# Running the first three weight blocks of an MLP over one half of the rows before the other half

## The chip, the cores and the metric

The kernel runs on one core of a Trainium2 chip. The metric is the device time of one execution in microseconds (us), as the median of several runs. The core has a matrix engine (TensorE, PE in the tables; its weight loads are listed apart as PEld), VectorE (DVE), ScalarE (ACT), GpSimd (POOL), and SyncE (SP), which issues the DMA transfers. Every engine works through its own queue in order.

## The reference

Four batches of 768 tokens with 384 features go through an attention-like recurrence, a real 2-D Fourier mix with layer norm, and two MLPs. Cut to what matters, for each batch:

```
y  = recurrence(q, k, v, a)                 # the scan and its attention form
u  = x + real(fft2(x))                      # x is y with its heads merged
un = layer_norm(u)
u  = u + relu(un @ w_ch1) @ w_ch2           # first MLP, 384 -> 1536 -> 384
u  = u + (relu(u.T @ w_tok1) @ w_tok2).T    # mix over the tokens
u  = u + relu(u @ w3) @ w4                  # second MLP, no layer norm
```

All is float32 at the interface. Each matrix is held as a high and a low part, and a product is three matmuls (high by high, low by high, high by low).

## The kernel before

Each batch is done by two strands of work. The **chain** is the scan (`scan`, mostly small VectorE steps and TensorE transposes at L642), the attention chunks (L753 to L810), and `stage2` (Fourier matmuls L1028 and L1039, the residual add L1091, layer norm L1098 to L1120). The **dense** strand is `mlp` (first MLP), `tok1` and `tok2` (the mix over tokens), `transposed`, and `mlp` again (second MLP). While the dense strand of batch b runs, the chain of batch b + 1 runs beside it. For batch 0 there is nothing to run beside the end of its chain. In the first dense pass the weights are also converted from the input form (`convert`, L185 to L207), which loads VectorE, GpSimd and ScalarE.

The program writes the strands one after the other with a priority on every instruction, and the scheduler that builds the program merges them into one fixed order for each engine, from these priorities and from what it takes to be ready. On TensorE the chain goes first and the dense work fills in; on VectorE, ScalarE and GpSimd the dense work goes first, conversions next, and the chain last. In each queue that order then holds, whatever the chip does.

A batch's 768 rows are six tiles of 128 rows. Layer norm finishes them in pairs: tiles 0 and 3, then 1 and 4, then 2 and 5 (L1118 on ScalarE, L1120 on VectorE). `transposed` takes them in the order 0, 3, 1, 4, 2, 5: three TensorE transposes for a tile (L906) into a PSUM bank of tag "s" (three banks), a ScalarE copy into the high part `th` (L909), and a VectorE subtraction for the low part `tl` (L910). `th` and `tl` have two halves of three tiles; before the change, half 0 holds tiles 0, 1, 2 and half 1 holds tiles 3, 4, 5.

`mlp` has four quarters. In a quarter, each of three weight blocks makes two groups of nine matmuls (L926), one for each half of the rows (384 columns); each group is evicted from a PSUM bank of tag "l" (three banks) by a ScalarE relu (L930) and a VectorE subtraction (L939), or for some by a second ScalarE relu and a GpSimd subtraction (L936, L937). Then six row tiles each take nine matmuls with the second weights (L948) and are added to `u` on VectorE (L951). Each weight tile is in one of four buffers for its tag ("w1" or "w2"), loaded at L283 in a fixed list. The hidden tiles `h` have three buffers.

The last batch is not run in that pattern: there the first MLP of batch 3 is interleaved with the token mix of batch 2 (`mixed`), and that stretch has no chain beside it any more.

Of the kernel before, what the change touches and what calls it, by code (L numbers as in the profile page):

```python
# [9 lines left out]
F32R = mybir.dt.float32r  # L10
I32 = mybir.dt.int32
U32 = mybir.dt.uint32
ACTF = mybir.ActivationFunctionType
# [40 lines left out]
def attn_fft_mixer_kernel(ctx: ExitStack, tc: tile.TileContext, aL, xL, vL, wL, qN, kN, vN, arN, aiN,  # L54
# [37 lines left out]
    def alloc(tag, shape, dt=F32, name=None):  # L92
        n = 1
        for x in shape[1:]:
            n *= x
        t = pool.tile([128, SIZE[tag]], dt, tag=tag, bufs=BUFS[tag], name=name or tag)
        return shaped(t[0:shape[0], 0:n], shape)
# [3 lines left out]
    def palloc(tag, shape):  # L101
        n = 1
        for s in shape[1:]:
            n *= s
        t = psum.tile([128, 512], F32, tag=tag, bufs=PSB[tag], name=tag)
        v = t[0:shape[0], 0:n]
        if len(shape) == 3:
            v = v.rearrange("p (a b) -> p a b", b=shape[2])
        return v

    def r32(ap):
        return ap.bitcast(F32)
# [786 lines left out]
    def transposed(u, un, pt):  # L899
        th = [alloc("T", [128, 3, 384], F32R, name="th") for _ in range(2)]  # L900
        tl = [alloc("T", [128, 3, 384], F32R, name="tl") for _ in range(2)]
        for i in range(6) if un is None else (0, 3, 1, 4, 2, 5):
            src = u[i] if un is None else un[:, i, :]
            px = palloc(pt, [128, 3, 128])
            for dt in range(3):
                te.transpose(px[:, dt, :], src[:, dt * 128:dt * 128 + 128], ident)  # L906
            o = (i % 3) * 128
            hi = th[i // 3][:, :, o:o + 128]
            se.copy(out=hi, in_=px)  # L909
            ve.tensor_tensor(out=tl[i // 3][:, :, o:o + 128], in0=px, in1=r32(hi), op=ALU.subtract)  # L910
        return th, tl

    def mlp(u, b, p0, th, tl, done):
        for qd in range(4):
            hs = []
            for m in range(3):
                p = p0 + 3 * qd + m
                w1 = ws.get(b, p, 0)
                h = alloc("h", [128, 2, 768], F32R, name="h")
                hs.append(h)  # L920
                for g in range(2):
                    ps = palloc("l", [128, 384])
                    n = 0
                    for kt in range(3):
                        for wi, x in ((0, th), (0, tl), (1, th)):
                            te.matmul(out=ps, lhsT=w1[:, wi, kt * 128:kt * 128 + 128],  # L926
                                      rhs=x[g][:, kt, :], start=(n == 0), stop=(n == 8))
                            n += 1
                    hi = h[:, 0, g * 384:g * 384 + 384]
                    x = se.activation(out=hi, in_=ps, func=ACTF.Relu)  # L930
                    marked(x)
                    lo = h[:, 1, g * 384:g * 384 + 384]
                    if done is None and 0 < b < B - 1 and m < 2:

                        full = alloc("f", [128, 384], name="full")
                        se.activation(out=full, in_=ps, func=ACTF.Relu)  # L936
                        ge.tensor_tensor(out=lo, in0=full, in1=r32(hi), op=ALU.subtract)  # L937
                    else:
                        ve.scalar_tensor_tensor(out=lo, in0=ps, scalar=0.0, in1=r32(hi), op0=ALU.max, op1=ALU.subtract)  # L939
                ws.ensure(b, p, 0, 2)  # L940
                yield True
            for tt in range(6):
                ps = palloc("l", [128, 384])
                n = 0
                for m in range(3):
                    w2 = ws.get(b, p0 + 3 * qd + m, 1)
                    for hi, wi in ((0, 0), (0, 1), (1, 0)):
                        te.matmul(out=ps, lhsT=hs[m][:, hi, tt * 128:tt * 128 + 128], rhs=w2[:, wi, :],  # L948
                                  start=(n == 0), stop=(n == 8))
                        n += 1  # L950
                ve.tensor_tensor(out=u[tt], in0=u[tt], in1=ps, op=ALU.add)  # L951
                if done is not None and qd == 3:
                    done(tt)
# [218 lines left out]
                    n += 1  # L1172
            ve.tensor_tensor(out=u[tt], in0=u[tt], in1=ps, op=ALU.add)

    def dense1(b, u, th, tl):
        go(mlp(u, b, 0, th, tl, None))
        R = tok1(b, u)
        tok2(b, u, *R)
        return transposed(u, None, "l")

    def mlp2(b, u, th, tl, row=None):
        def done(tt):
            sp.dma_start(out=out[b if row is None else bass.ds(row, 1), tt], in_=u[tt])
        return mlp(u, b, 16, th, tl, done)

    def dense2(b, u, th, tl, row=None):
        go(mlp2(b, u, th, tl, row))

    def mixed(g, b, u):

# [32 lines left out]
        u = u1  # L1223
    u1, norm = on(CHAIN, chain, B - 1)
    t3 = on(CHAIN, transposed, u1, norm, "s")
    on(DENSE, go, mlp(u, B - 2, 0, *t1, None))
    t2 = mixed(mlp(u1, B - 1, 0, *t3, None), B - 2, u)
    t3 = mixed(mlp2(B - 2, u, *t2), B - 1, u1)
    go(mlp2(B - 1, u1, *t3))

# [122 lines left out]
```

## Time and profile before

| what | value |
|---|---|
| median of 3 runs | 1102.06 us (1101.85 to 1102.67) |
| span of the profiled execution | 1097.6 us |
| time of the runs outside such a span (1102.06 - 1097.6) | 4.46 us |
| TensorE busy | 981.1 us, 89% |
| VectorE busy | 776.3 us, 71% |
| ScalarE busy | 511.7 us, 47% |
| GpSimd busy | 420.9 us, 38% |

The span runs from the first to the last instruction of one profiled execution. Busy shares are means over stages that have different limits, so they say only which engines are candidates. A matmul's end is modelled, so that its listed duration (some 0.33 us) is longer than the spacing of matmuls in a row.

### The profile page before, as it was taken

What the parts mean: (1) busy time and instruction counts of PE and PEld (TensorE: products, weight loads), DVE (VectorE), ACT (ScalarE), POOL (GpSimd) and SP (SyncE); (2) the same over time, 40 slices, a digit from 0 to 9 for tenths busy, and PEclk for the clock granted to TensorE, in tenths of its full rate; (3) what the DMA queues carried; (4) which work ended last, traced back from release to release, by engine and by line L of the source; (5) the groups of instructions that cost most, each with busy time, mean ns of one, the idle gap of its engine ahead of it and who ended that gap; (6) DMA issues with size and microseconds to landing.
All of it is one profiled execution on the core that took longest, in us unless ns stands there. A gap on an engine that the chain in (4) does not pass through costs nothing.

```text
span 1097.6 us, 21079 instructions
## 1 busy us (share of the span) xinstructions
PE 981.1 (89%) x7314; PEld 919.2 (84%) x7314; DVE 776.3 (71%) x2083; ACT 511.7 (47%) x1425; POOL 420.9 (38%) x552
## 2 busy tenths in 40 slices
PE   1358797999889989799998999999897999999997
PEld 0227675989889887799997899999786999999997
DVE  6986987999999668999758879984744433433332
ACT  6753355777877225968315556842234212121111
POOL 6643985573576454345336312424512002000000
PEclk9997797999999999799999999999998999999999
DMA  6136954686758663356664346664303433443432
GB/s 217 45 82 180 298 175 152 220 272 196 233 182 274 201 185 124 110 165 180 158 192 147 107 138 194 186 184 131 122 29 115 144 116 130 159 154 127 165 101 75
DMA packets 101537, 174.66 MB, mean 159 GB/s; under 512 B 11056, under 2 KB 61104, under 8 KB 100912
## 3 DMA queue, kind: packets, MB, share of 16 engines
q1 hardware_dynamic: 101424, 173.24, 51.1%
q8 instruction: 60, 0.98, 0.4%
q14 instruction: 53, 0.43, 0.1%
HBM read 133.88 MB, written 39.32 MB: 158 GB/s over the span
## 4 chain that ended last, share of the span: by engine, by line
PE 64%; DVE 10%; ACT 2%; DMA 2%; issue 1%; POOL 1%; SPq 0%; POOLq 0%; DVEq 0%; ACTq 0%
PE l L948 23%; PE l L926 21%; PE s L753 3%; PE s L642 2%; PE s L1039 2%; PE s L802 2%; DVE ws L994 2%; PE s L1028 1%; PE s L808 1%; PE s L1153 1%; PE s L768 1%; DVE ws L988 1%; PE s L1171 1%; DVE cvt L199 1%; PE s L906 1%
## 5 line engine op out<-in xcount | busy, mean ns | idle before, releaser
L948 PE MATMUL l<-w,h 128*128 128x384 f32 x1728 | 326.8, 340 | 5.7 <-DVE h L939 5.1
L926 PE MATMUL l<-th,w 128*128 128x384 f32 x1152 | 317.2, 344 | 8.8 <-DVE u L951 5.0
L948 PEld LDWEIGHTS l<-w,h 128*128 128x128 f32 x1728 | 298.4, 189 | 10.0 <-DVE h L939 7.2
L926 PEld LDWEIGHTS l<-th,w 128*128 128x128 f32 x1152 | 212.9, 191 | 13.3 <-DVE u L951 6.3
L926 PE MATMUL l<-tl,w 128*128 128x384 f32 x576 | 196.0, 340 | 3.6 <-DVE tl L910 3.6
L930 ACT ACTIVATE h<-l 128x384 fp32r<-128x384 f32 x192 | 94.0, 490 | 212.7 <-PE l L926 212.0
L951 DVE TENSOR_TENSOR u<-u,l 128x384 f32<-128x384 f32 x192 | 105.3, 549 | 81.9 <-PE l L948 80.9
L939 DVE SCALAR_TENSOR_TENSOR h<-l,h 128x384 fp32r<-128x384 f32 x160 | 88.4, 553 | 88.5 <-ACT h L930 88.3
L926 PEld LDWEIGHTS l<-tl,w 128*128 128x128 f32 x576 | 110.1, 191 | 4.1 <-DVE tl L910 4.1
L196 POOL TENSOR_TENSOR cvt<-cvt 128x384 int32<-128x384 int32 x56 | 64.7, 1160 | 36.7 <-DVE cvt L194 11.0
L466 PE MATMUL s<-misc,y 128*112 128x128 f32 x96 | 21.7, 369 | 53.1 <-DVE y L444 48.8
L466 PEld LDWEIGHTS s<-misc,y 128*112 128x112 f32 x96 | 14.0, 177 | 62.3 <-issue 26.8
L753 PE MATMUL s<-qkt 112*96 112x96 f32 x512 | 59.2, 266 | 6.7 <-DVE sc L760 6.7
L753 PEld LDWEIGHTS s<-qkt 112*96 112x96 f32 x512 | 53.2, 177 | 9.4 <-DVE sc L760 7.4
L1138 POOL TENSOR_TENSOR xl<-u,xh 128x384 fp32r<-128x384 f32 x18 | 17.9, 1006 | 105.6 <-ACT xh L1137 105.6
L206 POOL TENSOR_TENSOR w<-cvt,w 128x384 fp32r<-128x384 f32 x44 | 51.2, 1172 | 9.9 <-ACT w L205 6.1
L199 DVE SCALAR_TENSOR_TENSOR cvt<-cvt 128x384 int32<-128x384 int32 x56 | 48.1, 865 | 7.0 <-POOL cvt L196 6.8
L571 POOL TENSOR_TENSOR tm<-tm 128x144 f32<-128x144 f32 (+1 forms) x51 | 27.1, 531 | 59.0 <-ACT tm L570 58.7
L937 POOL TENSOR_TENSOR h<-full,h 128x384 fp32r<-128x384 f32 x32 | 33.6, 1049 | 35.5 <-ACT full L936 33.7
L642 PE MATMUL s<-misc,y 128*112 128x128 f32 x288 | 45.0, 276 | 1.4 <-DVE y L626 1.0
L615 DVE TENSOR_TENSOR p<-p,A 128x144 f32<-128x144 f32 x144 | 44.6, 310 | 2.2
L786 POOL TENSOR_TENSOR yc<-Aa,gm 48x384 f32<-48x384 f32 x18 | 21.0, 1164 | 63.3 <-DVE Aa L779 63.3
(234 smaller groups left out, 1950.8 us busy)
## 6 DMA issues: line engine op xcount, KB each, us to landing
w<-wscr SPq DMA_DIRECT2D x180, 384.0 KB, 3.5
cvt<-wL SPq DMA_DIRECT2D x56, 384.0 KB, 4.6
wscr<-w SPq DMA_DIRECT2D x44, 384.0 KB, 3.5
Kn<-kn SPq DMA_DIRECT2D x64, 192.0 KB, 3.7
kn<-y SPq DMA_DIRECT2D x96, 96.0 KB, 2.5
raw<-aL SPq DMA_DIRECT2D x48, 144.0 KB, 3.2
xx<-xL SPq DMA_DIRECT2D x48, 144.0 KB, 3.1
V<-vL SPq DMA_DIRECT2D x32, 144.0 KB, 3.1
```

What stands on the lines that cost most here:

```text
L196: x = ge.tensor_tensor(out=a, in0=a, in1=lo, op=ALU.add)
L199: rest(ve.scalar_tensor_tensor(out=a, in0=hi, scalar=-0x80000000, in1=a, op0=ALU.bitwise_and, op1=ALU.bitwise_or))
L206: ge.tensor_tensor(out=parts[:, 1, :], in0=a.bitcast(F32), in1=r32(parts[:, 0, :]), op=ALU.subtract)
L466: te.transpose(ps[:, j, :], y[:, j, 0:112], ident)
L615: ve.tensor_tensor(out=cur, in0=prev, in1=A[:, j, 0:3, :], op=ALU.mult)
L642: te.transpose(ps[:, j, :], y[:, j, 0:112], ident)
L753: te.matmul(out=ps[:, j, :], lhsT=K[:, hc, :], rhs=Q[:, hc, :])
L926: te.matmul(out=ps, lhsT=w1[:, wi, kt * 128:kt * 128 + 128], rhs=x[g][:, kt, :], start=(n == 0), stop=(n == 8))
L930: x = se.activation(out=hi, in_=ps, func=ACTF.Relu)
L939: ve.scalar_tensor_tensor(out=lo, in0=ps, scalar=0.0, in1=r32(hi), op0=ALU.max, op1=ALU.subtract)
L948: te.matmul(out=ps, lhsT=hs[m][:, hi, tt * 128:tt * 128 + 128], rhs=w2[:, wi, :], start=(n == 0), stop=(n == 8))
L951: ve.tensor_tensor(out=u[tt], in0=u[tt], in1=ps, op=ALU.add)
```

## The change

`transposed` fills the halves in the order in which layer norm delivers the tiles: where it follows layer norm, half 0 now holds tiles 0, 3, 1 and half 1 holds tiles 4, 2, 5. It also returns the `u` tiles in that order, and `mlp` adds its result to them in that order. With `halves=True` (the first MLP of batches 0, 1 and 2) the first quarter of `mlp` runs half 0 through its three weight blocks, and then half 1 through the same three blocks; the three hidden tiles are taken at its start. The first MLP of batch 3 keeps its order of blocks, with the new order of tiles. The numbers of matmuls, evictions, weight loads and stores stay as they are.

```diff
     def transposed(u, un, pt):
...
-        for i in range(6) if un is None else (0, 3, 1, 4, 2, 5):
+        order = range(6) if un is None else (0, 3, 1, 4, 2, 5)
+        for j, i in enumerate(order):
...
-            o = (i % 3) * 128
-            hi = th[i // 3][:, :, o:o + 128]
+            o = (j % 3) * 128
+            hi = th[j // 3][:, :, o:o + 128]
             se.copy(out=hi, in_=px)
-            ve.tensor_tensor(out=tl[i // 3][:, :, o:o + 128], in0=px, in1=r32(hi), op=ALU.subtract)
-        return th, tl
+            ve.tensor_tensor(out=tl[j // 3][:, :, o:o + 128], in0=px, in1=r32(hi), op=ALU.subtract)
+        return [u[i] for i in order], th, tl
 
-    def mlp(u, b, p0, th, tl, done):
+    def mlp(b, p0, u, th, tl, done, halves=False):
+        def up(p, h, m, g):
+            w1 = ws.get(b, p, 0)
+            ps = palloc("l", [128, 384])
...
         for qd in range(4):
             hs = []
+            first = halves and qd == 0
+            if first:
+                hs = [alloc("h", [128, 2, 768], F32R, name="h") for _ in range(3)]
+                for m in range(3):
+                    up(p0 + m, hs[m], m, 0)
             for m in range(3):
                 p = p0 + 3 * qd + m
...
+                if first:
+                    up(p, hs[m], m, 1)
+                else:
+                    hs.append(alloc("h", [128, 2, 768], F32R, name="h"))
+                    for g in range(2):
+                        up(p, hs[m], m, g)
...
-        go(mlp(u, b, 0, th, tl, None))
+        go(mlp(b, 0, uo, th, tl, None, True))
...
-    on(DENSE, go, mlp(u, B - 2, 0, *t1, None))
-    t2 = mixed(mlp(u1, B - 1, 0, *t3, None), B - 2, u)
+    on(DENSE, go, mlp(B - 2, 0, *t1, None, True))
+    t2 = mixed(mlp(B - 1, 0, *t3, None), B - 2, u)
```

The body of `up` (nine matmuls and the eviction) is the one that stood in the loop before.

## Rows read from the trace of the kernel before

**Rows 1.** The page: span, busy times, two groups of evictions, the weight loads

```profile
span 1097.6 us, 21079 instructions
PE 981.1 (89%) x7314; PEld 919.2 (84%) x7314; DVE 776.3 (71%) x2083; ACT 511.7 (47%) x1425; POOL 420.9 (38%) x552
...
L930 ACT ACTIVATE h<-l 128x384 fp32r<-128x384 f32 x192 | 94.0, 490 | 212.7 <-PE l L926 212.0
...
L939 DVE SCALAR_TENSOR_TENSOR h<-l,h 128x384 fp32r<-128x384 f32 x160 | 88.4, 553 | 88.5 <-ACT h L930 88.3
...
w<-wscr SPq DMA_DIRECT2D x180, 384.0 KB, 3.5
```

**Rows 2.** Windows: stretch, length, busy time (instructions) of each engine, clock, DMA

```profile
185.00:200.00 15.00, 14.59 (x71) 14.34 (x72) 10.91 (x30) 11.20 (x35) 7.57 (x13) 0.83 0.51 164
...
290.00:360.00 70.00, 63.64 (x410) 58.78 (x409) 67.81 (x186) 51.81 (x143) 44.78 (x53) 1.00 0.71 223
450.00:540.00 90.00, 90.00 (x591) 88.53 (x590) 81.97 (x276) 65.89 (x209) 42.12 (x70) 0.98 0.58 164
```

**Rows 3.** The chain that ended last, batch 1's stage 2: start, length, what

```profile
413.08 0.47 DVE u L951
...
419.66 0.23 DVE tm L577
...
424.23 2.53 PE s L1028 x24
```

**Rows 4.** The same chain near the program's end

```profile
1082.38 9.38 PE l L948 x54
```

**Rows 5.** Timeline, start of batch 0's first MLP: start, length, engine, operation

```profile
180.13 0.48 ACT L909 CAST th<-s 128x384 fp32r<-128x384 f32 x1 [0.16 <-PE s L906]
...
180.64 1.20 DVE L910 TENSOR_TENSOR tl<-s,th 128x384 fp32r<-128x384 f32 x2
...
183.24 1.51 PE L906 MATMUL s<-misc,ws 128*128 128x128 f32 x6 [2.50 <-DVE ws L1120]
...
185.41 1.39 PE L926 MATMUL l<-th,w 128*128 128x384 f32 x3 [0.66 <-ACT th L909]
```

**Rows 6.** Windows of that start, columns as in rows 2

```profile
185.00:190.00 5.00, 4.59 (x14) 4.34 (x15) 3.21 (x5) 3.88 (x13) 3.61 (x4) 0.50 0.42 141
```

**Rows 7.** Timeline, batch 0's last dense matmuls and batch 1's last layer-norm transposes

```profile
419.41 1.83 PE L948 MATMUL l<-w,h 128*128 128x384 f32 x9
...
445.65 1.54 PE L906 MATMUL s<-misc,ws 128*128 128x128 f32 x6 [1.80 <-ACT ws L1118]
...
446.59 0.48 ACT L909 CAST th<-s 128x384 fp32r<-128x384 f32 x1 [0.18 <-PE s L906]
...
447.73 1.54 PE L906 MATMUL s<-misc,ws 128*128 128x128 f32 x6 [0.53 <-ACT ws L1118]
```

**Rows 8.** Timeline, weight loads (SP's queue) and first matmul of batch 2's first MLP

```profile
630.71 7.92 SPq L283 DMA_DIRECT2D w<-wscr  x3
...
649.47 0.33 PE L926 MATMUL l<-th,w 128*128 128x384 f32 x1
```

**Rows 9.** Timeline, end of batch 3's layer norm

```profile
828.75 5.76 POOL L1138 TENSOR_TENSOR xl<-u,xh 128x384 fp32r<-128x384 f32 x6 [2.84 <-ACT xh L1137]
...
829.40 0.48 ACT L909 CAST th<-s 128x384 fp32r<-128x384 f32 x1
...
829.91 0.56 DVE L910 TENSOR_TENSOR tl<-s,th 128x384 fp32r<-128x384 f32 x1
...
832.67 0.92 DVE L1111 SCALAR_TENSOR_TENSOR rs<-mv,rs 128x2 f32<-128x2 f32 x1
...
834.58 0.16 DVE L1113 TENSOR_TENSOR rs<-rs 128x2 f32<-128x2 f32 x1
...
835.73 1.54 PE L906 MATMUL s<-misc,ws 128*128 128x128 f32 x6 [6.33 <-ACT ws L1118]
```

**Rows 10.** The chain that ended last, transposes of batch 2's layer norm

```profile
641.41 0.66 PE s L906 x6
```

## What the change should do to the time

> **What bounds the kernel now.** I read the page first: TensorE is busy 89% of the span, VectorE 71% [rows 1]. Both are means, so I next cut the span into stretches, and then walked the chain of waits. Three kinds of stretch matter. From 290 to 360 us VectorE has next to no pause (67.81 of 70 us) while TensorE has some (63.64) [rows 2]: the conversions, the dense evictions and batch 1's scan share it. From 450 to 540 us TensorE has no pause at all [rows 2]. Between them, in batch 1's attention and stage 2, the chain of waits runs from step to step: VectorE's steps with dense additions L951 among them, as at 413.08 with 0.47 us, scan 2's opening at 419.66, and only then the Fourier matmuls at 424.23 [rows 3]. After 836 us there is no chain left, and the dense work is a nearly unbroken TensorE stream to the end: 54 matmuls in 9.38 us, so 0.174 us each and 1.56 us for a group of nine [rows 4].
>
> So a saving counts at the end only if it brings forward a chain's end, or if it takes matmuls out of the tail. The change touches four places: the starts of the first MLP of batches 0 to 3.
>
> **Batch 0, the start itself.** TensorE transposes tiles 2 and 5 at 183.24 and starts the MLP at 185.41, after 0.66 us of waiting for tile 2's copy. The copy of tile 1 started at 180.13 and took 0.48 us; its low part is the first of two L910 that take 1.20 us from 180.64 [rows 5]. With the change, half 0 (tiles 0, 3, 1) is there at 180.61, and its low part about 0.6 us later. TensorE's pause of 2.50 us ahead of 183.24 and the 0.66 us ahead of 185.41 can both be filled: dense work of batch 0 is ahead by up to 3.2 us. At that point 14 matmuls take 4.59 us with the clock granted at 0.50, its lower level of 1.2 GHz, so 0.33 us each [rows 6]; the filled time holds nine or ten of them. It needs no more than 27, which is what half 0 has in three blocks.
>
> **What of it reaches the end.** Not the 3.2 us as such: batch 0's dense work ends with the nine L948 of 419.41, at 421.2 us, 26 us before batch 1's layer norm has given it the next tiles, at 447 [rows 7]. What counts is batch 1's chain. Two parts reach it. First, VectorE has 4.1 us of pause in 185 to 200 (10.91 busy of 15 [rows 2]), and 3.2 us of dense lead is 3.2 / 1.56 = 2.05 groups, with 0.553 us of VectorE each [rows 1]: 1.1 us of eviction moves into pauses, and the full stretch behind it ends that much sooner. Second, dense work then stands 3.2 - 1.1 = 2.1 us further on relative to the chain, or 1.3 groups, so that some 1.3 of the L951 additions leave stage 2's VectorE steps, at 0.47 us each on the chain [rows 3]: 0.6 us. Together 1.7 us. The bounds: 3.2 us if the chain keeps the whole lead; and a loss of 1.5 us if the fill does nothing and three relus of 0.49 us [rows 1] go ahead of scan 1's opening on ScalarE, where dense work has the priority. I take 1.7, since VectorE's pause in rows 2 is larger than the evictions that would go into it.
>
> **Batch 1.** Of the pauses before its transposes, 1.80 and 0.53 us are the last two, and only the last lies behind tile 1's copy (446.59 + 0.48 = 447.07) [rows 7]. The first MLP can fill it: 0.5 us, and nothing at the lower bound. This one counts in full, as the 90 us behind it have no TensorE pause.
>
> **Batch 2.** Its layer norm is over while the second MLP of batch 1 still occupies TensorE, so there is no pause to fill: 0. The blocks are wanted earlier, the third at group 3 in place of group 5. Three weight loads are issued within 7.92 us from 630.71, the last by 638.63, and with 3.5 us to landing [rows 1, 8] they are in by 642.1; the MLP starts at 649.47 [rows 8]. If that cover were gone, the wait would be at most one landing, 3.5 us. I take nothing. The fourth block's buffer comes free later, but is wanted a quarter later.
>
> **Batch 3.** TensorE waits 6.33 us before it transposes the last pair at 835.73, and tile 1's copies are done at 829.88 and 830.47 [rows 9]. Half 0 of the first block, nine matmuls, can go into that pause though `halves` is off here; before, it needed tile 2. That takes 1.56 us [rows 4] out of the tail. But its eviction enters VectorE's queue ahead of the last layer-norm steps, 0.56 us. So 1.0 us is left. The bounds are 0 (the scheduler leaves the order as it is) and 1.56 + 0.88 = 2.4, if the six transposes then run at the full clock, 0.66 in place of 1.54 us [rows 9, 10].
>
> Those layer-norm steps on two numbers a row take 0.92 us beside GpSimd's L1138, and 0.16 once it is over, while L910, which reads PSUM, takes 0.56 us beside L1138, at 829.91 [rows 9]. The Trainium skill, page "SBUF — State Buffer", section "SBUF: two separate sides", says that GpSimd and VectorE share a port pair as an exclusive lock, and that a VectorE operation takes part with two SBUF inputs or in a 2-port mode. L939 has one PSUM input, so by that rule it waits for nothing and the price stays 0.56; were it locked out like L1111, it would be 0.92, and this part 0.6 instead of 1.0.
>
> **Costed at nothing.** The numbers of matmuls, evictions and DMAs are unchanged. The order of the `u` tiles reaches `tok1`, which wants all of them. The three `h` buffers are free at each start: their last readers precede the MLP in TensorE's queue. If that were not so, a relu would wait for at most a group, 1.56 us.
>
> **The sum.** 1.7 + 0.5 + 0 + 1.0 = 3.2 us. The profiled execution spans 1097.6 us [rows 1]; with the 4.46 us that lie around it, it stands at the median of 1102.06. 1097.6 - 3.2 + 4.46 = 1098.9 us.
>
> **The rivals.**
>
> *The chain keeps the whole lead.* Batch 1's chain follows dense work through TensorE's queue and ends 3.2 us sooner, and batch 3 gives its 1.56 or more: 3.2 + 0.5 + 1.56 = 5.3 us, so 1096.8; with the upper bound of batch 3, 6.1 and 1096.0. For it: the order in TensorE's queue is fixed, so a queue that is ahead moves the chain's instructions too. Against it: VectorE is full up to 360 us [rows 2]. Chance 0.14.
>
> *The lead is hidden.* Batch 0 has 26 us of slack at 421, the relus push scan 1's opening back by up to 1.5 us, and this eats what batches 1 and 3 give, 1.5. So 1102.1, or from 1101 to 1103.6 with the bounds. This includes the case that the scheduler does not place half 0 ahead of the last transposes, so that the change does nothing. For it: rows 2; against it: VectorE's pauses in 185 to 200. Chance 0.27.
>
> *Slower: scan 2 moves further into stage 2 of batch 1.* In the chain of waits, scan 2's opening already stands between stage 2's VectorE steps and its Fourier matmuls, from 419.66 to 424.23, 4.57 us [rows 3]. If dense work is out of the way sooner, the scheduler can put as much again of scan 2 ahead of batch 1's layer norm. TensorE has no dense work from 421 to 447 [rows 7], and the lead that scan 2 gains is worth nothing behind it, where TensorE is the bound. Price 4.6, less batch 3's 1.0: 1105.7. It decides if more than about 3.7 us of scan 2 move ahead. Against it: the priorities do not change. Chance 0.15.
>
> **How the numbers follow.** The forecast case has 0.42, and 0.02 is left for what I have not seen. The time predicted is the forecast's, 1098.9; its own range is 1097.8 to 1100.2. The range for all is 1096.0 to 1104.0: it takes in the first rival down to its upper bound and the second up to its end, and leaves out the slower case. A difference of 0.2%, 2.2 us, is about what can be told from no change. Faster than 1099.9: 0.42 less a small part above, and 0.14, in all 0.55; same: 0.29; slower than 1104.3: 0.16.
>
> **What the profile would show.** Right: L926 starts near 180.7 ahead of the transposes of tiles 2 and 5, at the 0.50 clock; VectorE's busy time in 185 to 200 rises by a us; batch 0's last L948 ends some 3 us before 421, and batch 1's layer norm 1 to 2 us before 449; nine L926 stand before the last transposes near 835. Wrong: L926 still behind tile 2's transposes; batch 1's layer norm at the same time or later with more scan 2 steps before it; or a wait of L926 for a weight load near 650.

## The result, and the profile after

The changed kernel takes 1107.75 us (median of four runs, 1105.35 to 1110.44), the kernel before beside it 1102.09 (1101.85 to 1102.67): a ratio of 1.0051, with a 95% interval from 1.0031 to 1.0071. It is slower by 3.4 to 7.8 us. Predicted were 1098.9, and 1096.0 to 1104.0 as the range; the chance for "slower" was 0.16. Sign and size are wrong.

The profiled execution takes 1105.35 us and spans 1103.6 us, 6.0 us more than the 1097.6 us of before. Its page, to be read beside [rows 1]:

```profile
span 1103.6 us, 21059 instructions
...
PE 988.5 (90%) x7314; PEld 925.3 (84%) x7314; DVE 773.0 (70%) x2083; ACT 513.3 (47%) x1425; POOL 419.4 (38%) x552
```

TensorE is busy 7.4 us longer than before for the same 7314 matmuls, and VectorE 3.3 us less. The windows that answer to [rows 2] and [rows 6] (columns: length, then busy time and number of instructions of PE, PEld, DVE, ACT, POOL, then the granted clock, the DMA share and GB/s):

```profile
185.00:200.00 15.00, 13.23 (x70) 12.84 (x69) 10.57 (x30) 11.60 (x37) 7.19 (x13) 0.89 0.45 150
...
450.00:540.00 90.00, 88.96 (x541) 87.60 (x541) 78.10 (x267) 69.51 (x213) 43.45 (x73) 0.99 0.51 154
```

In 185 to 200 us VectorE is busy 10.57 us where it had been 10.91: the evictions that were to go into its pauses did not fill them. TensorE's unbroken stretch of 450 to 540 now has a gap (88.96 of 90).

Batch 0's start does what the change says. TensorE's timeline (start, length, tiles, count; in brackets the idle time ahead and what ended it), which answers to [rows 5]:

```profile
179.35 1.31 PE L923 MATMUL l<-th,w 128*128 128x384 f32 x3 [0.29 <-ACT th L910]
...
185.76 0.82 PE L907 MATMUL s<-misc,ws 128*128 128x128 f32 x6
188.35 0.79 PE L923 MATMUL l<-th,w 128*128 128x384 f32 x3 [1.77 <-ACT th L910]
```

The first MLP starts at 179.35, six us before the 185.41 of [rows 5], and all 27 matmuls of half 0 in three blocks stand ahead of the last two transposes, not the nine or ten that I had worked out. Three windows show the clock around this:

```profile
179.35:182.80 3.45, 3.45 (x11) 3.25 (x12) 2.52 (x10) 1.98 (x6) 0.03 (x1) 0.51 0.00 0
182.80:185.70 2.90, 2.90 (x18) 2.90 (x17) 1.56 (x4) 2.90 (x9) 1.96 (x3) 1.00 0.34 102
188.30:193.00 4.70, 4.65 (x17) 4.54 (x18) 2.48 (x8) 2.76 (x10) 3.49 (x7) 0.64 0.42 167
```

The granted clock is at its lower level of 1.2 GHz up to 182.8 and at 2.4 GHz (1.00) after it; then come six transposes and a wait of 1.77 us for half 1's copies, and the next 17 matmuls run at a mean of 0.64. The filled pause did not keep the clock up, and of the six us of earlier start 2.4 are left at the first matmul with the second weights (194.79 us, 197.17 before).

What the lead does to batch 1's scan stands on VectorE. From its first step of scan 1 to the first product `y` (L626) that TensorE waits for, the timelines of before and after read:

```profile
197.27 0.32 DVE L615 TENSOR_TENSOR p<-p,A 128x144 f32<-128x144 f32 x1
...
201.09 0.45 DVE L626 TENSOR_TENSOR y<-xx,p 128x288 f32<-128x288 f32 x1
```

```profile
197.90 0.32 DVE L615 TENSOR_TENSOR p<-p,A 128x144 f32<-128x144 f32 x1
...
206.68 0.44 DVE L626 TENSOR_TENSOR y<-xx,p 128x288 f32<-128x288 f32 x1
```

Both begin within 0.63 us of each other, but after the change the first product comes 5.59 us later. This is clear of chance: four kernels of the experiments (`early_b1`, `early_b1x`, `late_b1x`, `lay_b3`) have the order of before on VectorE, ScalarE and GpSimd up to 450 us, and in their traces it comes at 200.86 to 202.00. The groups of instructions of each stretch show what stands in between (count, busy time and mean ns of one):

```profile
L939 DVE SCALAR_TENSOR_TENSOR h<-l,h 128x384 fp32r<-128x384 f32 x2 | 1.1, 552 | 0.0
...
L951 DVE TENSOR_TENSOR u<-u,l 128x384 f32<-128x384 f32 x1 | 0.5, 546 | 0.0
```

```profile
L194 DVE TENSOR_SCALAR cvt<-cvt 128x384 int32<-128x384 int32 x4 | 2.5, 630 | 0.3 <-ACT cvt L191 0.3
L199 DVE SCALAR_TENSOR_TENSOR cvt<-cvt 128x384 int32<-128x384 int32 x2 | 1.9, 965 | 0.0
L963 DVE TENSOR_TENSOR u<-u,l 128x384 f32<-128x384 f32 x3 | 1.6, 542 | 0.0
```

Before, three evictions of dense work; after, three as well, but six steps of the weight conversions (L194 and L199, 2.5 + 1.9 us) have come ahead. The kernel ties each conversion's load to the relu written last (`hold`), and its result goes into a buffer that dense work has to leave first; so, as I read the kernel, a dense stream that is ahead brings conversions ahead too. I had left them out.

In batch 1 TensorE shows where the dense work stands. The first fence is before, the second after, both beside [rows 7]:

```profile
442.31 1.54 PE L906 MATMUL s<-misc,ws 128*128 128x128 f32 x6 [4.38 <-ACT ws L1118]
```

```profile
445.30 1.54 PE L907 MATMUL s<-misc,ws 128*128 128x128 f32 x6 [4.84 <-ACT ws L1130]
...
449.29 0.90 PE L907 MATMUL s<-misc,ws 128*128 128x128 f32 x3 [0.74 <-DVE tl L911]
449.85 1.31 PE L923 MATMUL l<-th,w 128*128 128x384 f32 x3
...
455.31 0.82 PE L907 MATMUL s<-misc,ws 128*128 128x128 f32 x6
455.97 0.49 PE L642 MATMUL s<-misc,y 128*112 128x128 f32 x3
```

```profile
456.50 0.45 DVE L626 TENSOR_TENSOR y<-xx,p 128x288 f32<-128x288 f32 x1 [3.10 <-PE s L642]
```

Its layer-norm transposes start 3.0 us late (445.30 against 442.31). Two traces do not give such a delay its size: in the four kernels just named, with the order of before up to there, these transposes start at 442.37, 446.32, 444.38 and 443.92. Then 24 MLP matmuls, the first of them again at the lower clock, stand ahead of the last transposes and of scan 2's first ones (L642) in TensorE's order, and VectorE waits 3.10 us for them: scan 2's first transposes come at 455.97. Before, they came at 449.28, right behind the last layer-norm transposes [rows 7]:

```profile
449.28 0.89 PE L642 MATMUL s<-misc,y 128*112 128x128 f32 x3
```

```profile
450.69 0.45 DVE L626 TENSOR_TENSOR y<-xx,p 128x288 f32<-128x288 f32 x1
```

This is scan 2's third product, and the first that has to wait for transposes, as the two before it have filled both of its buffers. It has moved from 450.69 to 456.50, by 5.8 us, of which 3.0 stood there already. The surest measure is taken within each trace, from batch 1's first layer-norm transposes to the last L615 of scan 2: 86.8 us before, 86.2 to 86.6 in the five kernels of the experiments that leave batch 1's tile order as it was and add no constraint there (`part_b0`, `lay_b0`, `lay_b0_v`, `lay_b3`, `halves_old`), and 93.1 with the change, 6.3 us more. Scan 2 ends at 538.4 and not at 529.2 (last L615), scan 3 at 740.4 and not 728.0, and batch 3's transposes start at 834.5 and not 826.9. From the last of them on the two runs go in step, and the end is 6.0 us later. At that place the change did next to nothing, beside [rows 9]:

```profile
841.84 0.69 PE L923 MATMUL l<-th,w 128*128 128x384 f32 x1
842.44 0.90 PE L907 MATMUL s<-misc,ws 128*128 128x128 f32 x3
```

One L923 comes ahead of the last three transposes, not nine.

### The profile page after: what moved, and what is told of

It reads as the page before. It is cut to its first block, busy times and chain, and to the rows that moved or that the text cites. A ratio compares the mean times of both kernels' runs of the same rounds, so it can differ in the third digit from the quotient of the medians.

```text
span 1103.6 us, 21059 instructions
## 1 busy us (share of the span) xinstructions
PE 988.5 (90%) x7314; PEld 925.3 (84%) x7314; DVE 773.0 (70%) x2083; ACT 513.3 (47%) x1425; POOL 419.4 (38%) x552
## 4 chain that ended last, share of the span: by engine, by line
PE 66%; DVE 17%; DMA 6%; ACT 4%; POOL 3%; issue 3%; SPq 1%; POOLq 0%; DVEq 0%; ACTq 0%
PE l L960 23%; PE l L923 22%; DMA cvt<-wL 4%; PE s L753 4%; PE s L1040 2%; PE s L642 2%; PE s L1051 2%; PE s L802 2%; DVE ws L1006 1%; PE s L808 1%; PE s L768 1%; DVE ws L1000 1%; PE s L1183 1%; PE s L1165 1%; DVE cvt L199 1%
## 5 line engine op out<-in xcount | busy, mean ns | idle before, releaser
L923 PE MATMUL l<-th,w 128*128 128x384 f32 x1152 | 320.8, 347 | 8.8 <-ACT th L910 3.1
L960 PEld LDWEIGHTS l<-w,h 128*128 128x128 f32 x1728 | 301.6, 190 | 19.1 <-DVE h L935 11.5
L923 PEld LDWEIGHTS l<-th,w 128*128 128x128 f32 x1152 | 212.8, 192 | 13.7 <-ACT th L910 4.3
L923 PE MATMUL l<-tl,w 128*128 128x384 f32 x576 | 196.9, 342 | 0.0
L923 PEld LDWEIGHTS l<-tl,w 128*128 128x128 f32 x576 | 110.4, 192 | 0.6 <-DVE tl L911 0.2
L199 DVE SCALAR_TENSOR_TENSOR cvt<-cvt 128x384 int32<-128x384 int32 x56 | 47.7, 859 | 6.4 <-POOL cvt L196 6.2
L642 PE MATMUL s<-misc,y 128*112 128x128 f32 x288 | 45.1, 273 | 3.8 <-DVE y L626 3.1
L615 DVE TENSOR_TENSOR p<-p,A 128x144 f32<-128x144 f32 x144 | 44.6, 310 | 2.2
L810 ACT ACTIVATE xT<-s,gate 112x384 f32<-112x384 f32 x24 | 13.9, 580 | 66.0 <-PE s L808 46.0
```

Source lines behind the costliest of these rows:

```text
L199: rest(ve.scalar_tensor_tensor(out=a, in0=hi, scalar=-0x80000000, in1=a, op0=ALU.bitwise_and, op1=ALU.bitwise_or))
L615: ve.tensor_tensor(out=cur, in0=prev, in1=A[:, j, 0:3, :], op=ALU.mult)
L642: te.transpose(ps[:, j, :], y[:, j, 0:112], ident)
L923: te.matmul(out=ps, lhsT=w1[:, wi, kt * 128:kt * 128 + 128], rhs=x[g][:, kt, :], start=(n == 0), stop=(n == 8))
```

## The experiments

The names used below: dense work is the two MLPs and what lies between them; a scan step's place is the number of dense matmuls that stand ahead of its transposes in TensorE's fixed order. All times are medians, with the ratio to the kernel before, run beside it, and its 95% interval; differences in us are worked out from that ratio. `after(x, y)` is the kernel's own way to say that x may not be placed ahead of y; it adds no wait on the chip by itself.

**Parts taken away.** The first four runs keep the new order of row tiles everywhere and switch the halves off, or on in one batch. The theories: W, batch 1's half 0 keeps scan 2 waiting; S, batch 0's lead slows scan 1 and the rest follows; R, any order laid anew costs.

```diff
-            first = halves and qd == 0
+            first = halves and qd == 0 and False         # tiles_only
+            first = halves and qd == 0 and b in (0, B)   # halves_b0; b in (1,) and b in (2,) likewise
```

> The new order of row tiles alone; no batch runs half 0 ahead of half 1. Theory W (batch 1's half 0 keeps scan 2's transposes L642 waiting): nine L926 stand ahead of batch 1's last transposes, not 24, so the time is that of the kernel before, 1100 to 1103 us. Theory S (batch 0's lead slows scan 1 and this compounds): the same, 1100 to 1103. Theory R (any re-laid order of the queues costs some us, wherever the change is): 1104 to 1109.

> New tile order, half 0 first in batch 0 alone. W: 1099 to 1103, as scan 2's transposes are again behind nine L926 only. S: 1105 to 1109, all of the loss, with scan 1 ending some 3 us late. R: 1104 to 1109.

> New tile order, half 0 first in batch 1 alone. W: 1105 to 1110, all of the loss; the first L642 after batch 1's layer norm comes some 6 us later than in the kernel before. S: 1100 to 1103. R: 1104 to 1109.

> New tile order, half 0 first in batch 2 alone, where the dense work before it still holds TensorE. W and S: 1100 to 1103, like the tile order alone. R: 1104 to 1109.

Measured: tile order alone 1118.17 us (1.0169, 1.0123 to 1.0215); with halves in batch 0 alone 1105.87 (1.0034, 1.0019 to 1.0048); in batch 1 alone 1124.08 (1.0176, 1.0134 to 1.0218); in batch 2 alone 1122.99 (1.0184, 1.0130 to 1.0238). W as stated is out: `halves_b0`, without halves in batch 1, still loses 3.7 us where W had nothing, and the others without them lose more. The tile order by itself costs more than the whole change, and halves in batch 0 give most of that back, which S had not expected. R stays open, though three of the four lie far above its 1104 to 1109. That scan 2 waits behind dense work comes back below, as the tile order alone also puts matmuls ahead of it.

**One batch, or one part, alone.** Three theories now: P, a scan step's place decides; L, the early start at the lower clock in batch 0 costs; N, the next batches cost.

```diff
 # lay_b0: tile order in batch 0 only, no halves
-            o = (j % 3) * 128
+            k = j if un is None or new else i          # new: layer norm of batch 0
+            o = (k % 3) * 128
 # halves_old: halves in every batch, tiles grouped as before
-            hi = th[j // 3][:, :, o:o + 128]
+            hi = th[i // 3][:, :, o:o + 128]
 # hold_b0, hold_b1: the changed kernel, and in that batch
+                    if n == 0 and done is None and p == 0 and g == 0 and b == 0:
+                        after(x0, ends[b])             # the last layer-norm transpose
```

> No halves anywhere, and the new order of row tiles in batch 0 alone; batches 1 to 3 as in the kernel before. Theory P (place in the queue): what counts is how many dense matmuls stand ahead of each scan step in TensorE's fixed order. Here steps 24 to 30 of scan 1 have 45 to 53 more of them ahead than before, 8 to 9 us of TensorE, and from scan 2 on the order is that of before. So scan 1 ends 8 to 15 us late, dense work of batch 0 runs out some 5 us earlier, TensorE idles by the difference before batch 1's layer norm is over, and most of that stays: 1110 to 1118. Theory N (the next batches): the 16 us of the tile order alone come from the nine matmuls ahead of the transposes in batches 1 and 3, and batch 0 is absorbed by its 26 us of slack: 1102 to 1104.

> The changed kernel, with batch 0's first MLP matmul held behind the last transpose after layer norm. TensorE's order in batch 0 is then that of before up to the end of scan 1 (at most 17 matmuls more ahead of a step), while in batch 1 there are still up to 24 matmuls ahead of the last transposes or of scan 2, and 9 to 36 more ahead of the steps of scan 2. Theory P: scan 1 ends as before (346 to 348), and what is left is batch 1's share, half of the loss: 1104 to 1105. Theory L (the early start at the lower clock in batch 0 is what costs): 1102. Theory N (batch 1 is what costs): 1107 to 1108, as the changed kernel.

> The changed kernel, with batch 1's first MLP matmul held behind the last transpose after layer norm: no dense matmul ahead of batch 1's transposes, and the first three scan steps of batch 1 come ahead of it, as before. Batch 0 as in the changed kernel. Theory P: scan 1 ends as in the changed kernel (349); the steps of scan 2 have 9 to 36 more matmuls ahead than before, against 27 to 54 in the changed kernel: half of the loss, 1104 to 1105.5. Theory N: 1102 to 1103. Theory L: 1107 to 1108.

> The halves stay, the order of row tiles is undone: half 0 is tiles 0, 1, 2, of which tile 2 comes fifth. TensorE's order is then that of the kernel before, except for which weight block the first six groups of a batch read, and for at most 9 matmuls ahead of a scan step. Theory P: 1102, within 1101 to 1103. If the halves themselves cost (blocks wanted sooner, h buffers, conversions held behind a later relu), 1104 or more with a wait of the MLP for a weight load or a conversion.

Measured: `halves_old` 1102.04 (0.9998, 0.9981 to 1.0016), `hold_b0` 1105.97 (1.0050, 1.0024 to 1.0076), `hold_b1` 1106.84 (1.0041, 1.0024 to 1.0057), `lay_b0` 1122.85 (1.0197, 1.0163 to 1.0232). The halves cost nothing that can be told, to 2 us, where the order stays (to 9 matmuls ahead of a scan step): blocks wanted sooner, the three `h` buffers and the later hold of a conversion are free, as I had costed them. The tile order in batch 0 alone loses as much as in every batch. And taking away the early matmuls of one batch alone does not bring the time back: L and N by themselves are out, and the half that P gives lies below both medians, if not below both intervals.

For `lay_b0` the reason can be read on VectorE. Its groups from 185 us to the end of scan 1 (346.95 before, 360.0 here):

```profile
L199 DVE SCALAR_TENSOR_TENSOR cvt<-cvt 128x384 int32<-128x384 int32 x33 | 28.4, 862 | 1.9 <-POOL cvt L196 1.7
L939 DVE SCALAR_TENSOR_TENSOR h<-l,h 128x384 fp32r<-128x384 f32 x36 | 19.7, 548 | 0.6 <-ACT h L930 0.5
...
L194 DVE TENSOR_SCALAR cvt<-cvt 128x384 int32<-128x384 int32 x32 | 14.4, 453 | 0.1
```

```profile
L199 DVE SCALAR_TENSOR_TENSOR cvt<-cvt 128x384 int32<-128x384 int32 x36 | 30.7, 852 | 1.6 <-POOL cvt L196 1.4
L940 DVE SCALAR_TENSOR_TENSOR h<-l,h 128x384 fp32r<-128x384 f32 x41 | 22.4, 547 | 1.0 <-ACT h L932 1.0
...
L194 DVE TENSOR_SCALAR cvt<-cvt 128x384 int32<-128x384 int32 x36 | 18.1, 502 | 4.3 <-ACT cvt L191 4.1 <-POOL cvt L196 0.2
```

Five more evictions (L940, 41 for 36) and seven more conversion steps (72 for 65) are done before scan 1's end, 2.7 + 2.3 + 3.7 = 8.7 us of VectorE in a stretch where it is full, and it waits 4.1 us for the conversions' first step on ScalarE. Scan 1 ends 13 us late.

**The place of the scan steps, shifted in the kernel before.** None of these four has both parts of the change in batch 1: `part_b0` has the change in batch 0 alone, and the others are the kernel before with one constraint. Theory T says that the tile order, the halves or the early matmuls cost by themselves, B that the order of before is a balance from which both directions cost.

```diff
 # early_b1: scan 2's first transposes behind batch 1's third MLP group
+                    if b == 1 and p == 1 and g == 0 and done is None:
+                        after(begins[2][0], z)
 # late_b0 (late_b1x): the batch's first MLP matmul behind scan transposes
+                            if b == 0 and p == 0 and g == 0 and n == 0 and done is None:
+                                after(z, steps[1][5])       # late_b1x: b == 1, steps[2][11]
```

> The kernel before, tile order and halves untouched; one ordering constraint is added: the first scan step's transposes of scan 2 stand behind the third group of batch 1's first MLP (27 matmuls). From there on the fixed order has 9 to 36 more dense matmuls ahead of the steps of scan 2 and 18 to 36 more ahead of those of scan 3, the same numbers as in the kernel with batch 1 held; scan 1 and batch 0 are those of before, and no matmul stands ahead of a layer norm's transposes. Theory P (the place of scan steps behind dense work is what costs): 1105 to 1107, as the four variants with that order. Theory T (tile order, halves or the early matmuls among the transposes cost by themselves): 1102, within 1101 to 1103.

> The change in batch 0 alone: tile order and halves there, and everything of batches 1 to 3 as in the kernel before. Scan 1 has 9 to 36 more dense matmuls ahead of its steps up to the ninth group and as many as before at its end; from scan 2 on the order is that of before, to 18 matmuls. Theory P: scan 1 ends up to 3 us late, most of it hidden by the time that TensorE waits before batch 1's layer norm is over, or kept: 1102 to 1105. Theory L (the start at the lower clock costs): 1106 or more. My prediction's own step for batch 0: 1100.4.

> The kernel before with one constraint in the other direction: batch 0's first MLP matmul stands behind the sixth transpose group of scan 1. Scan 1's steps then have up to 200 fewer dense matmuls ahead of them, those of scan 2 and 3 10 to 54 fewer. Theory P taken as a line (4 us for 27 matmuls): scan 1 ends well before 346, and 1096 to 1100. Theory B (the order of before is a balance: dense work left out of TensorE's waits beside scan 1 comes back at the end): 1104 to 1115, with TensorE waiting between 185 and 215.

> The kernel before with batch 1's first MLP matmul behind the twelfth transpose group of scan 2, as against the first. 36 to 100 fewer dense matmuls stand ahead of the steps of scan 2 and 60 to 100 fewer ahead of those of scan 3. Theory P as a line: scan 2 and attention 2 end 8 to 15 us sooner, and the time is 1092 to 1098. Theory B: TensorE waits for VectorE's scan steps from 449 on, dense work of batch 1 starts some 15 to 20 us later, and the time is 1104 to 1115.

Measured: `early_b1` 1107.40 (1.0049, 1.0026 to 1.0072), `part_b0` 1104.16 (1.0018, 1.0001 to 1.0036), `late_b0` 1109.95 (1.0078, 1.0048 to 1.0108), `late_b1x` 1109.40 (1.0075, 1.0047 to 1.0103). `early_b1` is the clearest run of the study. It has neither tile order nor halves, and up to batch 1's last layer-norm transposes it goes as the kernel before:

```profile
447.78 1.54 PE L912 MATMUL s<-misc,ws 128*128 128x128 f32 x6 [0.53 <-ACT ws L1126]
449.55 1.39 PE L932 MATMUL l<-th,w 128*128 128x384 f32 x3 [0.22 <-ACT th L915]
...
455.01 1.14 PE L644 MATMUL s<-misc,y 128*112 128x128 f32 x9
```

```profile
455.58 0.44 DVE L628 TENSOR_TENSOR y<-xx,p 128x288 f32<-128x288 f32 x1
```

There are 19 MLP matmuls between 449.55 and 455.01. Scan 2's third product is 4.9 us late (455.58 against 450.69), the stretch from the first layer-norm transposes to scan 2's end is 3.9 us longer (90.7 against 86.8), and the kernel is 5.4 us slower (2.9 to 7.9). So the delay of scan 2, with what the order lays behind it, is still there at the end, and within the intervals it costs as much as the whole change. The other direction costs as well: with batch 0's dense work held back TensorE waits for scan 1's products, and with batch 1's for scan 2's, as the lists of TensorE's waits show (what for, us in total, times, longest):

```profile
PE s L644 <- DVE y L628: 20.2, 4, 14.4
```

```profile
PE s L644 <- DVE y L628: 6.2, 2, 3.1
```

The kernel before waits for them next to nothing in its whole run, as its page says:

```profile
L642 PE MATMUL s<-misc,y 128*112 128x128 f32 x288 | 45.0, 276 | 1.4 <-DVE y L626 1.0
```

So P as a line is out, and both times lie in B's range of 1104 to 1115: 20.2 and 6.2 us of TensorE's time are lost there. In `late_b0` scan 1 ends 23 us sooner (last step 323.6 against 346.6), and the kernel is 8.6 us slower all the same: an early end of the scan that is paid for with TensorE's time is worth nothing.

**The places pinned.** If the place on TensorE were the whole cause, pinning every scan step to its place of before should bring the time back under the whole change.

```diff
 # pinned; pinned_b1 (batches 1 and 2 only), lay_b0_pinned (on lay_b0)
+    def pin(x, b, second, n):                      # x: first matmul of a dense group
+        at = 936 * b + 504 * second + 9 * n        # its number in the dense work
+        k = [i for i, q in enumerate(PLACE) if q <= at]   # PLACE: of the kernel before
...
+                after(x, steps[k[-1]])
 # early_b1x: scan 2's third transpose group behind batch 1's sixth MLP group
+                        after(begins[2][2], z)
```

> The whole change (tile order and halves in every batch), with one kind of constraint added: no dense group may stand ahead of a scan step that it stood behind in the kernel before. The places of all 96 scan steps are then those of before within 9 matmuls, while 27 matmuls still stand ahead of batch 0's last two transposes and nine ahead of batch 3's. Theory P, the place is the whole cause: 1101 to 1103. If what I predicted for batches 0 and 3 is real besides, once the order is kept: 1099 to 1101. Theory T (early matmuls, halves or tile order cost by themselves): 1105 to 1108, as the changed kernel.

> The same, but batch 0's dense groups are not pinned: scan 1's steps have 9 to 36 more matmuls ahead than before up to the ninth group, as in the changed kernel, and scans 2 and 3 have their places of before. Theory P: the pinned kernel's time plus batch 0's share, 2 us by the kernel with the change in batch 0 alone: 1103 to 1105. If the shares do not add up (batch 1 absorbs what batch 0 loses): the pinned kernel's time.

> The tile order in batch 0 alone, which cost 20 us, with scan steps pinned as above. The steps of scan 1 then have up to 63 fewer matmuls ahead than before in its second half in place of 45 to 53 more; everything from scan 2 on is as before. Theory P: the 20 us are gone, and what is left is at most the price of the other direction (7 us for 200 fewer): 1101 to 1106. Theory T (the nine early matmuls or the order of row tiles cost by themselves): 1115 to 1125.

> The kernel before, with scan 2's third transpose group behind the sixth dense group of batch 1 in place of scan 2's first behind the third. Scan 2's first two groups stay where they were; from the third on 36 to 45 more matmuls stand ahead than before at first, then 24 to 45, and in scan 3 33 to 48, some 9 more than in the other kernel. Theory P: more than the other's 4.7 us, 5 to 9: 1107 to 1111. If only the first scan step counts: 1102.

Measured: `pinned` 1119.38 (1.0155, 1.0140 to 1.0169), `pinned_b1` 1109.13 (1.0056, 1.0040 to 1.0071), `lay_b0_pinned` 1113.64 (1.0108, 1.0091 to 1.0125), `early_b1x` 1106.69 (1.0036, 1.0024 to 1.0048). P falls here: all places are kept to some ten matmuls, and it costs 17 us. Nor does the loss go away with the places of batches 1 and 2 alone: in `pinned_b1` the stretch from batch 1's first layer-norm transposes to scan 2's end is down to 88.2 us from the 93.1 of the change, and the kernel still costs 6.2 us (4.4 to 7.8). The slope is not there either: `early_b1x` puts more matmuls ahead than `early_b1`, from the third group of steps on, and costs no more (4.0 us, 2.6 to 5.3). The rows of `pinned` on TensorE and VectorE say what else there is:

```profile
196.15 6.41 PE L980 MATMUL l<-w,h 128*128 128x384 f32 x36
209.36 0.86 PE L654 MATMUL s<-misc,y 128*112 128x128 f32 x3 [6.81 <-DVE y L638]
```

```profile
208.76 0.44 DVE L638 TENSOR_TENSOR y<-xx,p 128x288 f32<-128x288 f32 x1
```

TensorE reaches the first scan step's place by 202.6, and waits 6.81 us for a product that VectorE ends at 209.2: on VectorE evictions and conversions still stand ahead of it, as in the changed kernel. So the place on TensorE is not all of it; the order on VectorE has to fit too.

**VectorE's order pinned, and batch 3 by itself.** The last two runs test that on the variant with the largest loss, and the one step of my prediction that no kernel had carried out.

```diff
 # lay_b0_v: on lay_b0; EV, C1, C2 are the counts ahead of scan 1's steps in the kernel before
+                    behind(v, EV)         # each eviction of batch 0 (L939, L951)
+        behind(x, C1)                     # each conversion step L194
+        behind(x, C2)                     # each conversion step L199
 # lay_b3: as lay_b0, for the layer norm of batch 3
```

> The tile order in batch 0 alone, which cost 20 us, with another kind of constraint: on VectorE, no dense eviction and no weight conversion of batch 0's pass may stand ahead of a step of scan 1 that it stood behind in the kernel before. TensorE's order then follows: the steps of scan 1 have at most 10 more matmuls ahead than before in place of up to 53, scans 2 and 3 have the same as before, and nine matmuls still stand ahead of batch 0's last two transposes. Theory V (VectorE's fixed order decides: evictions and conversions that come ahead of a scan step push scan 1 back, as the rows show, 5 evictions and 7 conversion steps more before its end): scan 1 ends near 347 and the 20 us are gone: 1101 to 1105. Theory T (the nine early matmuls, or the order of row tiles itself, cost): 1115 to 1125. In between, 1108 to 1114, if TensorE waits for the scan as in the kernel with scan steps pinned on TensorE.

> The tile order in batch 3 alone, no halves. The order of everything up to batch 3's layer norm is that of the kernel before; there nine first-MLP matmuls come ahead of the last two transposes, which the whole change did not bring about (one matmul there). This is my prediction's step for batch 3 by itself: 1.0 us less, 1101, with bounds 0 and 2.4. Theory R (any order laid anew costs): 1104 or more. If the saved 1.56 us go into later pauses: 1102.

Measured: `lay_b0_v` 1106.28 (1.0050, 1.0036 to 1.0065, without its longest execution), `lay_b3` 1101.94 (1.0012, 1.0001 to 1.0023). With VectorE's order in batch 0 pinned, three quarters of the 21.7 us are gone (5.5 are left, more than the 1101 to 1105 of theory V), though the same nine matmuls stand ahead of the transposes and the row tiles have the same order. TensorE's order follows that of VectorE here, so the two are not wholly apart; pinning TensorE's places alone had taken less off (`lay_b0_pinned`, 11.9 us left). VectorE's groups up to scan 1's end, now at 350.2, have the counts of before again:

```profile
L216 DVE SCALAR_TENSOR_TENSOR cvt<-cvt 128x384 int32<-128x384 int32 x33 | 29.0, 882 | 1.4 <-POOL cvt L213 1.4
L964 DVE SCALAR_TENSOR_TENSOR h<-l,h 128x384 fp32r<-128x384 f32 x36 | 19.6, 547 | 0.9 <-ACT h L956 0.9
...
L209 DVE TENSOR_SCALAR cvt<-cvt 128x384 int32<-128x384 int32 x32 | 13.3, 422 | 0.7 <-ACT cvt L206 0.7
```

`lay_b3` leaves all of the order up to batch 3 as it was. Nine matmuls go ahead there, and the layer norm comes later by nearly as much as they take. On TensorE:

```profile
830.14 0.55 PE L911 MATMUL s<-misc,ws 128*128 128x128 f32 x3 [0.31 <-DVE tl L916]
...
838.48 1.54 PE L911 MATMUL s<-misc,ws 128*128 128x128 f32 x6 [5.20 <-ACT ws L1135]
839.67 3.55 PE L1170 MATMUL s<-xh,w 128*128 128x384 f32 x10
```

From the transposes ahead of the pause to the last ones it is 838.48 - 830.14 = 8.34 us, where it was 835.73 - 828.84 = 6.89 [rows 9], 1.45 more. I had counted the one eviction among the layer-norm steps, and it is there at its price (0.54 us on VectorE at 835.50, beside GpSimd's L1155, which runs from 831.69 to 837.47). What I had not counted is ScalarE, where the layer norm's second step (L1108, here L1125) has slipped behind three more casts:

```profile
831.38 0.31 ACT L1107 ACTIVATE rs<-mv,lnc 128x2 f32<-128x2 f32 x1
831.72 0.20 ACT L1108 ACTIVATE rs<-rs 128x2 f32<-128x2 f32 x1
```

```profile
832.34 0.29 ACT L1124 ACTIVATE rs<-mv,lnc 128x2 f32<-128x2 f32 x1
832.54 1.32 ACT L1154 CAST xh<-u 128x384 fp32r<-128x384 f32 x3
833.77 0.20 ACT L1125 ACTIVATE rs<-rs 128x2 f32<-128x2 f32 x1
```

That is 1.43 us between the two steps in place of 0.34. Behind the pause the first ten L1170 then take 3.55 us where they took 2.85:

```profile
836.92 2.85 PE L1153 MATMUL s<-xh,w 128*128 128x384 f32 x10
```

## Why the prediction was wrong

**The steps that failed** are "What of it reaches the end" and "Batch 1"; the second weighs more. In the first I saw that the lead itself was worth nothing, as batch 0's dense work has 26 us of slack, and then gave it two ways into batch 1's chain, both with the sign of a gain: 1.1 us of evictions into VectorE's pauses, and 0.6 us of additions out of stage 2. Measured alone (`part_b0`), batch 0's part is a loss of 2.0 us (0.1 to 4.0) where I had a gain of 1.7. On VectorE dense evictions go ahead of the scan, and the weight conversions came ahead with them, so scan 1's first product comes 5.59 us later. How the loss at the end comes of that is not shown. The delay is gone by the fourteenth product (327.21 against 327.46), and up to scan 1's end (185 to 349.85 us) VectorE has done as many evictions and conversion steps as before, to one (the rows of before stand at `lay_b0`):

```profile
L935 DVE SCALAR_TENSOR_TENSOR h<-l,h 128x384 fp32r<-128x384 f32 x35 | 19.2, 548 | 2.6 <-ACT h L927 2.5
...
L194 DVE TENSOR_SCALAR cvt<-cvt 128x384 int32<-128x384 int32 x33 | 17.8, 539 | 1.1 <-ACT cvt L191 0.9
```

The evictions wait 2.6 us for ScalarE in place of 0.6, and a conversion's first step takes 539 ns in place of 453. Scan 1's last step starts at 349.5, where the five traces with the order of before have 346.6 to 348.8. Pinning VectorE's order takes three quarters of the loss out where counts did differ, with the tile order in batch 0 alone; with the whole change it was not run. The pauses that I wanted to fill were not there to be filled: in 185 to 200 us the longest, 2.0 us, is the scan's own wait for GpSimd, as it was before (2.1), the evictions waited 1.4 us for ScalarE's relus (0.5 before), and VectorE was busy 0.34 us less, not 1 us more. And the lead was 2.4 us and not 3.2, with the lower clock met twice.

**Batch 1** I had at -0.5, "in full". The sign was wrong. The pause was filled, but with 24 matmuls, 5.5 us of them, and behind the pause there stood more than two transposes: scan 2's first transposes are next in TensorE's order, and VectorE and the rest of the chain wait for those. In the changed kernel's own trace the stretch up to scan 2's end is 6.3 us longer than before. `early_b1` shows that such an order costs this much by itself: 4.9 us of delay there, and 5.4 us at the end. Holding the early matmuls of batch 1 back (`hold_b1`) leaves 4.5 us (2.6 to 6.3); there the later steps of scan 2 still stand 9 to 36 matmuls further back than before. What is not shown is that the loss goes away with this order: `pinned_b1` mended the stretch, and not the time. The two shares, 2.0 and 5.4, add up to 7.4; measured for the change are 5.6 (3.4 to 7.8). They were not measured in one kernel, so that they add up is not shown.

**Batch 2** at nothing was right as to the blocks: no wait for a weight load near 650, and `halves_old` shows that the halves' buffers and loads are free.

**Batch 3** at -1.0 did not take place in the changed kernel, since the order there was laid with one matmul ahead (my lower bound, 0). Where it does take place (`lay_b3`) it costs 1.3 us (0.1 to 2.5). The price of the eviction was right, but ScalarE's order (1.45 us with the eviction) and the slower start behind the pause (0.70 us) are more than the 1.56 us that were to be saved; and from the last transposes to the end of the span it is 261.9 us in both profiles, so the saving itself does not show.

**The sum** took 4.46 us for time outside the span. Every listed execution leaves 1.4 to 2.2 us there; the rest is that the profiled execution of before was some 2.7 us faster than the median (an estimate from these numbers). In the sum it cancels out.

**The rivals.** The slower rival had a lead of dense work turned into a longer way to batch 1's layer norm, for 1105.7. Its sign was right and its mechanism was not: scan 2 did not move ahead of the layer norm, it was pushed behind dense work. That an order laid anew costs on its own account, wherever it starts, was no rival of mine, and of the eighteen kernels of the experiments, the seventeen whose order differs by more than that of `halves_old` were all slower, by 1.3 to 21.7 us, the two smallest (1.3 and 2.0) barely clear of nothing.

**What stays open.** Why the kernel with all places pinned costs 17 us where the change without pins costs 5.6 (from batch 0's first layer-norm transposes to batch 1's it takes 281.5 us, where the five traces with the order of before take 266.6 to 269.9); what the 5.5 us are that remain with VectorE's order pinned; where the time of `pinned_b1` goes; and whether the change with both orders pinned would gain anything. No kernel that was run beats the kernel before.

## What to carry to other kernels

Where two streams share engines under a fixed order, a pause that is filled with one stream's work can move that work ahead of the other stream on every engine it passes through, with what is tied to it (here evictions and weight conversions): ask first which stream sets the end, and count what then stands ahead of its next step on each engine. Before an edit is blamed, shift the order in the unchanged kernel by one constraint: here that cost as much as the whole edit, and the one part that could be run with next to no shift, the halves, cost nothing that could be told. And before a delay is read off one trace against another, see how far traces of the same order differ: here by 4 us at batch 1's layer norm, and by 0.6 us in the stretch from there to scan 2's end.

## What was not expected of the hardware

The same instruction of VectorE takes different times in different kernels, and no run isolates why: the mean of the conversions' L194 went from 453 ns in the kernel before to 539 in the changed kernel, 502 in `lay_b0` and 422 in `lay_b0_v`, each from 185 us to the end of scan 1. The clock, once at 1.00, fell back behind a pause of 1.77 us that followed six transposes (0.64 over the next 4.7 us). One of the five executions of `lay_b0_v` took 3816.77 us; no trace of it exists, its cause is open, and the median stands with it.
